# Moving the load of f to the head of the program and pinning twelve GpSimd loads in program order

## The chip, the cores and the metric

The kernel runs on one core of a Trainium2 chip. A core has TensorE (PE: matmuls, with its weight loads listed apart as PEld), VectorE (DVE), ScalarE (ACT), GpSimd (POOL) and SyncE (SP), each with a queue of its own that it works through in order, and sixteen DMA engines that all queues share. The metric is the device time of one execution in microseconds (us); lower is better.

## The reference

Inputs: q, k, v of shape (8, 8, 576, 64) for batch, head, position and head size; f of shape (8, 8, 576); w_in (512, 2048) and w_out (2048, 512).

```python
scores = q @ k.T / sqrt(64)
cum    = cumsum(log(clip(f, 1e-4, 1)), axis=-1)
scores = where(causal, -1e9, scores + cum[:, :, :, None] - cum[:, :, None, :])
attn   = softmax(scores) @ v
x      = attn with heads side by side, as 4608 tokens of 512
h      = x @ w_in
g      = h where h >= 1; 0 where h <= -1; (h + 1)**2 / 4 between
out    = g @ w_out
```

So the work is attention with a decay for each head, then two dense layers over all tokens.

## The kernel before

**Precision.** Later batches and the dense layers work on float16 pairs: a number is scaled by a power of two, its high part kept in one float16 and the rest in another, and a product takes three matmuls. The scale has to be known first: it comes from the largest absolute value of a whole batch of q, k or v. The first jobs work in float32 and need fewer scales.

**Jobs.** Attention is cut into 36 jobs, each two heads of one batch. Batch 0 has eight: its four head pairs with row blocks 0 and 1 (jobs 0 to 3), then with row blocks 2 to 4 (jobs 4 to 7). Batches 1 to 7 have four jobs each, with all five row blocks: batch 1 is jobs 8 to 11, batch 2 begins with job 12. Jobs below `NPE` = 8 turn their weights with PE in float32; jobs below `NQK` = 12 take q and k in float32, and from job 12 on q and k are split by a scale (`prepare`, L379).

**Loop.** The main loop (L737) walks the jobs. In job p it loads job p + 2, prepares job p + 1, and for each row block computes scores (`scores`, L443: PE writes them into PSUM, POOL lays out decay and causal mask at L474 and L478), the softmax (`weights`, L542: DVE takes the minimum at L556, ACT the exponential at L560, both split the result) and, in the second step, the product with v for the job before (`values`, L588, or `early_values`, L516). Between the steps it works off weight blocks (`weight_step`, L715: eight blocks of w_in and w_out are loaded by SP, their bits moved on DVE at L196 to L202, scaled and split; all in jobs 1 to 6) and units of the dense layers (`moe_unit`, L690: 256 tokens by one of eight weight blocks, 144 units in all). A unit can run only when all its tokens are through attention: chunk 0 after job 3, chunk 1 after job 7, chunks 2 and 3 after job 11.

**Start.** `decay_sums` (L140) loads f into the tile `early`, clips it on DVE (L144), takes the logarithm on ACT (L147), the running sum on DVE (L150), and stores it to DRAM as `cum_d`; `load_decay` (L369) reads it back, one row broadcast over all partitions. In the program, the load of f stands behind the loads of job 0's q and k (L362), all on SP's queue.

**The scales.** `value_scale(b)` (L236) loads a batch of v in four parts of 288 KB into `vm`, takes the largest absolute value of each on DVE (L245), and has `across` (L111) turn the result over the partitions with PE. `query_scale(b)` (L261) does it for q and k in eight parts (L268, L269). Batch 0's v is loaded by SP into another tile; all other parts are loaded by POOL into `vm`, which has two buffers that are used in program order: 28 loads for v of batches 1 to 7 and 48 for q and k of batches 2 to 7. In the program, `value_scale(1)` stands in job 7 behind the scores of its row block 4, and `query_scale(2)` in job 9 behind the scores of row block 1; v of batch 2 follows in job 11, q and k of batch 3 in job 13, and so on.

`across` uses the PSUM tile `s`, which has one buffer and is also that of the scores of row blocks 0 to 3. So this last step of a scale stays where the program has it, between two row blocks. The loads and the reductions before it do not: the small tiles that hold their results (`m4`, `m8`, `m1`, `m2q`, two buffers each) let them run some batches ahead.

**What sets the order.** The kernel is written for a scheduler (the context is opened with `schedule_with_timeline_sim=True`). It takes the instructions in the order in which the program issues them, simulates the engines, and fixes for each engine the order of its queue: an instruction whose inputs and buffers are free in that simulation may be put far ahead of its place in the program. On the chip each queue is then worked off in that fixed order, so an instruction that waits holds up everything behind it on its engine. `tc.keep_in_program_order(load)`, which the change calls, adds one condition to this: the load must be queued behind the instruction that the program issued last on the same engine before it. It is a condition of order alone; nothing waits for anything to end.

Of the kernel before, what the change touches and what calls it, by code (L numbers as in the profile page):

```python
# [30 lines left out]
NQK = 12  # L31
# [14 lines left out]
def kernel(  # L46
# [20 lines left out]
    nc = tc.nc  # L67

    B, H, S, D = q.shape
# [23 lines left out]
    early = xpool.tile([P, NPAIR, 2, S], F16, name="x").rearrange("p a b s -> p (a b s)").bitcast(F32)  # L93
# [11 lines left out]
    def scale_of(scale, power, m):  # L105

        nc.vector.tensor_scalar(out=power, in0=m, scalar1=1.0 / TOP, scalar2=None, op0=ALU.mult)
        even_pow2(power, power)
        nc.vector.reciprocal(scale, power)

    def across(dst, m):  # L111

        n = m.shape[1]
        pt = ps1.tile([P, 2, 512], F32, name="s")[:, 0]
        nc.tensor.transpose(pt[0:n, 0:P], m, ident)
        top = tiny.tile([P, 1], F32, name="top", bufs=2)  # L120
        nc.vector.tensor_reduce(out=top[0:n], in_=pt[0:n, 0:P], axis=AX.X, op=ALU.max)
        nc.vector.tensor_scalar(
            out=top[0:n], in0=top[0:n], scalar1=LOW, scalar2=HIGH, op0=ALU.max, op1=ALU.min
        )
        dg = tiny.tile([P, 2], F32, name="dg", bufs=2)
        nc.vector.tensor_scalar(
            out=dg[0:n, 0:n], in0=ident[0:n, 0:n], scalar1=top[0:n], scalar2=None, op0=ALU.mult
        )
        nc.tensor.matmul(pt[:, P:P + n], lhsT=ones[0:n], rhs=dg[0:n, 0:n], start=True, stop=True)
        nc.vector.tensor_copy(dst, pt[:, P:P + n])  # L130
# [6 lines left out]
    cum_d = dram.tile([B * H, S], F32, name="cum_d")  # L137
    cq8 = const.tile([P, NT5, B * H], F32, name="cq8")

    def decay_sums():  # L140
        fl = early
        nb = B * H
        nc.sync.dma_start(fl[0:nb, 0:S], f.rearrange("b h s -> (b h) s"))
        nc.vector.tensor_scalar(  # L144
            out=fl[0:nb, 0:S], in0=fl[0:nb, 0:S], scalar1=1e-4, scalar2=1.0, op0=ALU.max, op1=ALU.min
        )
        nc.scalar.activation(fl[0:nb, S:2 * S], fl[0:nb, 0:S], AF.Ln)  # L147
        nc.gpsimd.memset(fl[0:nb, 3 * S:4 * S], 0.0)
        cum = fl[0:nb, 2 * S:3 * S]
        nc.vector.tensor_tensor_scan(  # L150
            out=cum, data0=fl[0:nb, S:2 * S], data1=fl[0:nb, 3 * S:4 * S], initial=0.0, op0=ALU.add, op1=ALU.add
        )
        nc.sync.dma_start(cum_d, cum)
        pt = ps1.tile([P, 1024], F32, name="big")
        twice = fl[0:nb, 0:P]
        nc.vector.tensor_copy(
            twice.rearrange("p (a b) -> p a b", a=2), cum[:, FULL:S].unsqueeze(1).broadcast_to([nb, 2, 64])
        )
        for t in range(NT5):
            nc.tensor.transpose(  # L160
                pt[:, nb * t:nb * t + nb], cum[:, P * t:P * t + P] if t < LAST else twice, ident[0:nb, 0:nb]
            )
        nc.vector.tensor_scalar(
            out=cq8.rearrange("p t n -> p (t n)"), in0=pt[:, 0:NT5 * nb], scalar1=8.0, scalar2=None, op0=ALU.mult
        )
# [70 lines left out]
    def value_scale(b):  # L236
        m4 = tiny.tile([P, NPAIR], F32, name="m4", bufs=2)
        for i in range(NPAIR):
            if b:
                st = two.tile([P, S], F32, name="vm")  # L240
            else:
                st = stage[:, i * S:(i + 1) * S]
            part = v[b, 2 * i:2 * i + 2].rearrange("h s d -> (h s d)").rearrange("(p n) -> p n", p=P)
            (nc.gpsimd if b else nc.sync).dma_start(st, part)
            nc.vector.tensor_reduce(  # L245
                out=m4[:, i:i + 1], in_=st, axis=AX.X, op=ALU.max, apply_absolute_value=True
            )
        m1 = tiny.tile([P, 1], F32, name="m1", bufs=2)
        nc.vector.tensor_reduce(out=m1, in_=m4, axis=AX.X, op=ALU.max)
        m = mv[:, b:b + 1]  # L250
        across(m, m1)
        if b:
            nc.vector.tensor_tensor(out=m, in0=m, in1=mv[:, b - 1:b], op=ALU.max)
        scale_of(sv[:, b:b + 1], pv[:, b:b + 1], m)
# [6 lines left out]
    def query_scale(b):  # L261

        ms = tiny.tile([P, 2, NPAIR], F32, name="m8", bufs=2)
        for j, src in enumerate((q, k)):
            for i in range(NPAIR):
                st = two.tile([P, S], F32, name="vm")
                part = src[b, 2 * i:2 * i + 2].rearrange("h s d -> (h s d)").rearrange("(p n) -> p n", p=P)
                nc.gpsimd.dma_start(st, part)  # L268
                nc.vector.tensor_reduce(  # L269
                    out=ms[:, j, i:i + 1], in_=st, axis=AX.X, op=ALU.max, apply_absolute_value=True  # L270
                )
        m2 = tiny.tile([P, 2], F32, name="m2q", bufs=2)
        nc.vector.tensor_reduce(out=m2, in_=ms, axis=AX.X, op=ALU.max)
        mk = tiny.tile([P, 2], F32, name="mk", bufs=2)
        across(mk, m2)
        sc = sqk[:, :, b]
        scale_of(sc, mk, mk)
        nc.vector.tensor_scalar(
            out=nsig[:, b:b + 1], in0=sc[:, 0:1], scalar1=sc[:, 1:2], scalar2=-8.0, op0=ALU.mult, op1=ALU.mult
        )  # L280
        nc.vector.reciprocal(nalpha[:, b:b + 1], nsig[:, b:b + 1])
        nc.vector.tensor_scalar(
            out=cqs[b % 2], in0=cq8[:, :, b * H:(b + 1) * H], scalar1=nsig[:, b:b + 1], scalar2=-0.125,
            op0=ALU.mult, op1=ALU.mult,
        )
# [442 lines left out]

    pairs = [load(0)]
    decay_sums()  # L730
    pairs.append(load(1))
    load_decay(pairs[0], 0)
    load_decay(pairs[0], 1)
    prepare(pairs[0])
    value_scale(0)
    split_values(pairs[0])
    for p in range(njobs + 1):  # L737
# [3 lines left out]
        if w:  # L741
            if w.b not in xs:
                xs[w.b] = xpool.tile([P, NPAIR, 2, S], F16, name="x")
            if p + 2 < njobs:
                pairs.append(load(p + 2))
            if nxt:
                load_decay(nxt, 0)
                prepare(nxt)
            scores(w, w.r0)

            def step(r):
                if r + 1 < w.r1:
                    scores(w, r + 1)
                if r == w.r0 and w.hp == 1 and w.b + 1 < B and p + 3 >= NQK:
                    query_scale(w.b + 1)
                if r == w.r1 - 2 and nxt:
                    load_decay(nxt, 1)
                    if nxt.hp == 0 and nxt.r0 == 0:
                        value_scale(nxt.b)
                    split_values(nxt)  # L760
                weights(w, r)

            steps = [lambda r=r: step(r) for r in range(w.r0, w.r1)]
# [60 lines left out]
```

## Time and profile before

| what | value |
|---|---|
| median of 3 runs | 1199.87 us (1199.61 to 1200.08) |
| the profiled execution | 1195.69 us, its span 1193.9 us |
| PE | 1064.8 us busy, 89% |
| DVE | 806.8 us, 68% |
| ACT | 770.4 us, 65% |
| POOL | 476.1 us, 40% |
| mean granted clock of PE | 0.951 |
| loads into `vm` by POOL | 76, of 288 KB each |

The span runs from the first to the last instruction of the profiled execution; the time of an execution has a little more around it. Busy time counts an engine's own work, not its waiting or the issuing of transfers. In a row of a timeline stand the start, the duration, the engine, the line, the operation, the tiles (written <- read) and the shapes, the count, and in brackets how long the engine had been idle and what ended that. A row of waits has the waiting instruction, what it waited for, the total in us, how often, and the longest. In the rows of slices each digit is the busy share of a fortieth of the span in tenths; PEclk is the clock granted to PE in the same way. A chain of waits that the page follows from the last instruction back covers only the last 300 us here, which is dense work on PE; the first 330 us are therefore read by stretches.

### The profile page before, as it was taken

To read this page: it belongs to the slowest core of one execution; us is meant where nothing else is said; L and a number is where in the kernel's file an instruction comes from. 1 tells how busy PE (TensorE), PEld (TensorE's weight loads), DVE (VectorE), ACT (ScalarE), POOL (GpSimd) and SP (SyncE) were. 2 spreads that over 40 slices of the span, in tenths; PEclk is the share of its full clock that TensorE was granted. 3 is DMA by queue.
4 is the path that set the end of the run, shared out by engine and by line. 5 is a ranking of instruction groups with operands and counts; after the bars stand their busy time and mean duration, and the time that the engine had idled before them with its cause. 6 is when DMAs were issued, how large, how long until landed. Compare 5 with 4: busy or idle time off the path is not lost. (4 is left out here: it accounts for less than half of the span.)

```text
span 1193.9 us, 24608 instructions
## 1 busy us (share of the span) xinstructions
PE 1064.8 (89%) x8871; PEld 681.6 (57%) x8871; DVE 806.8 (68%) x2140; ACT 770.4 (65%) x1599; POOL 476.1 (40%) x811
## 2 busy tenths in 40 slices
PE   2566766998689899999999999999999999999998
PEld 1334443655356556655666665565566666677665
DVE  5979878777778777768656666777767866522222
ACT  2756555758567767777667666786777776644443
POOL 3588643534464544544432232454434444000000
PEclk9767888999789999999999999999999999999999
DMA  8797744689989977867665555777767773300000
GB/s 269 220 296 210 216 138 143 134 192 162 181 159 201 188 132 161 153 137 147 123 115 103 108 111 116 149 157 139 141 129 146 128 130 66 74 19 2 19 18 18
DMA packets 392537, 162.60 MB, mean 136 GB/s; under 512 B 370016, under 2 KB 371040, under 8 KB 392416
## 3 DMA queue, kind: packets, MB, share of 16 engines
q1 hardware_dynamic: 377312, 115.03, 49.4%
q0 software_dynamic: 9920, 36.58, 10.8%
q10 hardware_dynamic: 5184, 9.44, 2.3%
q8 instruction: 69, 1.13, 0.4%
q14 instruction: 52, 0.43, 0.1%
HBM read 89.80 MB, written 9.58 MB: 83 GB/s over the span
## 5 line engine op out<-in xcount | busy, mean ns | idle before, releaser
L637 PE MATMUL ph<-x,place 128*128 128x256 f16 (+3 forms) x4608 | 430.3, 248 | 10.1 <-DVE u L648 8.0
L665 PE MATMUL po<-place,g 128*128 128x512 f16 x1728 | 412.8, 382 | 4.1 <-ACT g L650 3.9
L637 PEld LDWEIGHTS <-place 128*128 128x128 f16 x4608 | 355.4, 99 | 85.4 <-issue 29.2
L474 POOL TENSOR_SCALAR sdr<-ck,nsig,cqs 128x128 f32<-128x128 f32 (+1 forms) x192 | 154.3, 808 | 297.7 <-DVE pr L575 278.5
L665 PEld LDWEIGHTS <-g 128*128 128x128 f16 x1728 | 162.3, 98 | 176.9 <-issue 8.3
L560 ACT ACTIVATE sdr<-sdr,nm 128x128 f32<-128x128 f32 (+1 forms) x240 | 132.6, 553 | 75.8 <-DVE nm L556 75.1
L648 DVE SCALAR_TENSOR_TENSOR u<-ph,z,u 128x512 f32<-128x512 f32 x136 | 101.5, 746 | 107.0 <-ACT u L647 106.7
L646 ACT ACTIVATE u<-ph,z 128x512 f32<-128x512 f32 x136 | 104.4, 768 | 80.0 <-PE ph L637 78.1
L650 ACT ACTIVATE g<-u,z 128x512 f16<-128x512 f32 x136 | 97.8, 719 | 71.0 <-DVE u L648 67.1
L575 DVE SCALAR_TENSOR_TENSOR pr<-sdr,rc,pr 128x128 f16<-128x128 f32 (+1 forms) x224 | 116.3, 555 | 39.9 <-ACT pr L574 37.7
L651 DVE SCALAR_TENSOR_TENSOR g<-u,z,g 128x512 f16<-128x512 f32 x136 | 104.2, 766 | 48.1 <-ACT g L650 47.6
L574 ACT ACTIVATE pr<-sdr,rc 128x128 f16<-128x128 f32 (+1 forms) x224 | 112.6, 550 | 18.9 <-ACT sdr L560 14.3
L556 DVE CUSTOM_DVE_ANT_0 sdr<-s,sdr,nalpha 128x128 f32<-128x128 f32 (+1 forms) x192 | 98.4, 546 | 26.5 <-PE s L466 16.2
L466 PE MATMUL s<-qkT 64*128 64x128 f16 (+5 forms) x704 | 88.3, 347 | 26.7 <-DVE nm L556 23.9
L595 PE MATMUL big<-pT,vs 128*64 128x64 f16 (+3 forms) x1008 | 83.8, 291 | 18.6 <-DMA pT<-pr 10.8
L647 ACT ACTIVATE u<-u 128x512 f32<-128x512 f32 x144 | 89.8, 624 | 2.5
L478 POOL TENSOR_SCALAR_AFFINE_SELECT sdr<-sdr 128x128 f32<-128x128 f32 x240 | 85.0, 363 | 7.8
L595 PEld LDWEIGHTS <-vs 128*64 128x64 f16 x1008 | 53.1, 113 | 51.6 <-issue 33.2
L474 POOL TENSOR_SCALAR sd<-ck,nsig,cqs 64x576 f32<-64x576 f32 x48 | 47.0, 980 | 78.9 <-DMA ck<-cum_d 60.5
L466 PEld LDWEIGHTS <-qkT 64*128 64x128 f16 (+1 forms) x864 | 32.8, 99 | 59.7 <-issue 46.1
L390 DVE SCALAR_TENSOR_TENSOR qs<-qk,sqk,qs 128x640 f16<-128x640 f32 x48 | 42.4, 910 | 30.8 <-ACT qs L389 30.8
L389 ACT ACTIVATE qs<-qk,sqk 128x640 f16<-128x640 f32 x48 | 37.3, 820 | 38.8 <-DMA qkT<-qs 33.2
(163 smaller groups left out, 1140.3 us busy)
## 6 DMA issues: line engine op xcount, KB each, us to landing
ck<-cum_d POOLq DMA_DIRECT2D x48, 288.0 KB, 4.5
out_dram<-ot ACTq DMA_DIRECT2D x36, 256.0 KB, 3.5
qk<-in_k_dram SPq DMA_DIRECT2D x64, 128.0 KB, 3.1
vm<-in_v_dram POOLq DMA_DIRECT2D x28, 288.0 KB, 3.5
v<-in_v_dram SPq DMA_DIRECT2D x56, 128.0 KB, 3.0
qk<-in_q_dram SPq DMA_DIRECT2D x56, 128.0 KB, 2.8
vm<-in_q_dram POOLq DMA_DIRECT2D x24, 288.0 KB, 3.4
vm<-in_k_dram POOLq DMA_DIRECT2D x24, 288.0 KB, 3.4
```

Source lines behind the costliest of these rows:

```text
L466: nc.tensor.matmul(outs[h][:, c0:c1], lhsT=x[rows], rhs=y[rows, c0:c1], start=(i == 0), stop=(i == len(terms) - 1),)
L474: nc.gpsimd.tensor_scalar(out=sd[p0:p1, 0:wid], in0=w.ck[h][p0:p1, 0:wid], scalar1=w.nsig if w.p < NQK else w.nsig[p0:p1], scalar2=w.cqs[p ...
L556: nc.vector.tensor_tensor_reduce(out=a, in0=sp, in1=a, scale=w.nalpha, scalar=BIG, op0=ALU.add, op1=ALU.min, accum_out=nm[:, i:i + 1],)
L560: nc.scalar.activation(a, a, AF.Exp, bias=nm[:, i:i + 1], scale=-1.0, accum_out=sm[:, i:i + 1])
L574: nc.scalar.activation(pr[:, :, 0, i, :], a, AF.Copy, scale=rc[:, i:i + 1])
L575: nc.vector.scalar_tensor_tensor(out=pr[:, :, 1, i, :], in0=a, scalar=rc[:, i:i + 1], in1=pr[:, :, 0, i, :], op0=ALU.mult, op1=ALU.subtract,)
L595: nc.tensor.matmul(av[64 * h:64 * h + 64, at + s0:at + s1], lhsT=w.vs[:, vl, h, t, :], rhs=w.pT[:, t, pl, h, s0:s1], start=(t == 0 and pi ...
L637: nc.tensor.matmul(ph[:, fi, a0:a1], lhsT=wi[fb][:, wl, t, fi * P:(fi + 1) * P], rhs=xs[b][:, t, xl, s0:s0 + a1 - a0], start=(fi == 0 and ...
L646: nc.scalar.activation(u, h, AF.Relu, scale=z.u[:, i:i + 1], bias=z.h[:, i:i + 1])
L648: nc.vector.scalar_tensor_tensor(out=u, in0=h, scalar=z.t[:, i:i + 1], in1=u, op0=ALU.max, op1=ALU.min)
L651: nc.vector.scalar_tensor_tensor(out=g[:, 1], in0=u, scalar=z.r[:, i:i + 1], in1=g[:, 0], op0=ALU.mult, op1=ALU.subtract)
L665: nc.tensor.matmul(po[ch][i], lhsT=g[:, gl, fi * TC + i * P:fi * TC + (i + 1) * P], rhs=wo[fb][:, wl, fi, :], start=(first and fi == 0 and ...
```

## The change

The load of f is issued as the first transfer of the program, ahead of the q and k of job 0. And twelve of the 76 loads into `vm` get the condition above: the four of v of batch 1, and the eight of q and k of batch 2 (`4 * (b + 1) == NQK` holds for b = 2). The other 64 are left to the scheduler, which lays out the order of all queues anew. Nothing is computed that was not computed before.

```diff
+    nc.sync.dma_start(early[0:B * H, 0:S], f.rearrange("b h s -> (b h) s"))
+
     def decay_sums():
         fl = early
         nb = B * H
-        nc.sync.dma_start(fl[0:nb, 0:S], f.rearrange("b h s -> (b h) s"))
...
-            (nc.gpsimd if b else nc.sync).dma_start(st, part)
+            load = (nc.gpsimd if b else nc.sync).dma_start(st, part)
+            if b == 1:
+                tc.keep_in_program_order(load)
...
-                nc.gpsimd.dma_start(st, part)
+                load = nc.gpsimd.dma_start(st, part)
+                if 4 * (b + 1) == NQK:
+                    tc.keep_in_program_order(load)
```

## The prediction

> **What bounds the kernel now.** I read the page first: the forty slices, then busy time by stretch.
>
> ```profile
> span 1193.9 us, 24608 instructions
> PE   2566766998689899999999999999999999999998
> DVE  5979878777778777768656666777767866522222
> PEclk9767888999789999999999999999999999999999
> ```
>
> One slice is 29.85 us. PE is far from full in the first seven slices, dips again in the eleventh, and is full from the twelfth on. Cut there:
>
> ```profile
> 0.00:223.00 223.00, 137.20 (x746) 89.51 (x747) 173.88 (x499) 124.24 (x304) 130.43 (x204) 0.82 0.71 210
> 223.00:334.00 111.00, 95.61 (x723) 57.01 (x720) 84.30 (x239) 73.76 (x159) 51.07 (x96) 0.92 0.87 169
> 334.00:1050.00 716.00, 692.63 (x6269) 439.83 (x6266) 508.52 (x1349) 511.54 (x1051) 294.64 (x512) 0.99 0.69 132
> 1050.00:1194.00 144.00, 139.32 (x1141) 95.22 (x1139) 40.09 (x54) 60.85 (x87) 0.00 (x0) 1.00 0.04 16
> ```
>
> (Stretch, its length, then busy us of PE, weight loads, DVE, ACT, POOL; granted clock; DMA share; GB/s.) From 334 us PE is busy 832.0 of 860 us: that part is as long as its matmuls. Before 334 us PE idles 101.2 us (334 - 137.2 - 95.6). So the run ends earlier or later by about as much as the attention of batches 0 and 1, which feeds PE, finishes earlier or later. In the first 223 us DVE is the fullest engine, 173.9 us. What the change moves is work of DVE, POOL and DMA in these two stretches: the `vm` loads and the reductions behind them.
>
> ```profile
> 0.00:100.00 100.00, 8.79 (x12) 7.61 (x13) 0.78 0.86 258
> 100.00:223.00 123.00, 29.84 (x40) 23.16 (x41) 0.85 0.59 172
> 223.00:330.00 107.00, 8.80 (x12) 6.83 (x12) 0.92 0.86 169
> 330.00:450.00 120.00, 8.87 (x12) 5.70 (x10) 0.94 0.84 170
> 2.64 1.27 POOL L244 DMA_DIRECT2D vm<-in_v_dram  x2
> 223.08 0.53 DVE L537 SCALAR_TENSOR_TENSOR x<-big,sv,x 128x320 f16<-128x320 f32 x1
> ```
>
> The first four rows are the same view for `vm` alone (busy us and count on DVE, then POOL). All 76 reductions are done by 450 us: 12, 40, 12, 12. Loads for batches that are attended hundreds of us later run ahead, the first pair at 2.64 us, and 40 of the reductions fall into the stretch at whose end, 223 us, batch 0 is finished (L537, the last step of job 7).
>
> **The change part by part.** The sum is made against the profiled execution: 1195.69 us, of which the span is 1193.9. It is 4.18 us under the median of the three runs, 1199.87; I add that at the end.
>
> *Load of f.*
>
> ```profile
> 0.75 0.97 SPq L362 DMA_DIRECT2D qk<-in_q_dram  x2
> 1.77 0.97 SPq L362 DMA_DIRECT2D qk<-in_k_dram  x2
> 2.79 0.57 SPq L143 DMA_DIRECT2D x<-in_f_dram  x1
> 7.59 0.45 DVE L144 TENSOR_SCALAR x<-x 64x576 f32<-64x576 f32 x1 [7.59 <-DMA x<-in_f_dram]
> 11.65 0.69 PE L408 MATMUL big<-ident,qk 128*128 128x128 f32 x2 [0.58 <-DVE cq L163]
> ```
>
> f moves past four loads of q and k on SP's queue, from 2.79 to 0.75 us: 2.04 us earlier, and DVE, which has done nothing until then, starts by as much earlier. The four loads go out 0.57 us later; the first transpose, which needs them, was released by DVE (cq) and not by them, so this is covered, unless f gains so much that q and k are next late. Taken: -2; ends 0 (the weight split on DVE, whose own loads stand behind on SP, is next late) and -4 (f's 4.8 us of landing shortens as well, since it no longer shares the engines with four loads).
>
> *The pinned loads: where they go.* A load of batch 1's v may now not stand ahead of the POOL instruction traced just before it, the last mask of row block 4 of job 7; the loads of q and k of batch 2 stand behind the second mask of row block 1 of job 9. Both can be found in POOL's timeline:
>
> ```profile
> 116.18 0.24 POOL L478 TENSOR_SCALAR_AFFINE_SELECT sd<-sd 64x64 f32<-64x64 f32 x1
> 235.03 0.29 POOL L478 TENSOR_SCALAR_AFFINE_SELECT sdr<-sdr 128x128 f32<-128x128 f32 x1
> ```
>
> So v of batch 1 starts at about 116 us, not at 2.64, and q and k of batch 2 at about 235. No other load is pinned, but all use the two `vm` buffers in program order, so all of them queue behind those twelve: none of the other 64 can start before about 250 us.
>
> *The first 100 us* lose 12 loads: 8.79 us of DVE, and POOL's waits for a buffer. DVE's longest waits there are not for them:
>
> ```profile
> DVE x L144 <- DMA x<-in_f_dram: 7.6, 1, 7.6
> DVE place L228 <- ACT place L223: 3.3, 2, 2.2
> DVE u L196 <- DMA place<-in_moe_w_out_dram: 3.2, 1, 3.2
> ```
>
> (Who waits for what, us in total, times, longest.) Ends 0 and -8.8; taken -2, near the first, because DVE's gaps there come from other work.
>
> *100 to 223 us* lose 40 reductions and get v's four.
>
> ```profile
> 100.00:223.00 123.00, 90.11 (x548) 59.32 (x549) 98.48 (x291) 71.06 (x162) 67.24 (x103) 0.85 0.59 172
> DVE m L269 <- DMA vm<-in_q_dram: 6.8, 5, 3.0
> DVE m L245 <- DMA vm<-in_v_dram: 4.3, 7, 1.6
> DVE m L269 <- DMA vm<-in_k_dram: 1.6, 4, 0.7
> ```
>
> DVE is busy 98.5 of 123 us, and stood still 12.7 us (6.8 + 4.3 + 1.6) at a reduction whose load had not landed, with the softmax and weight steps of batch 0 queued behind it. Reductions and stalls hold DVE 42.5 us. The gain is at most PE's idle time, 32.9 us (123 - 90.1), since PE's work stays; at least nothing. Taken: the stalls, 12.7, and a quarter of the 29.8 us of reductions (most fill time that DVE had to spare): -20. That is 0.5 us for each load. What is next late are the steps that PE waits for, exp and scaling on ACT. v's four loads cost 4 x 0.5 = +2.
>
> *Job 9.* The maxima of q and k of batch 2 are turned across partitions in the PSUM tile `s`, which has one buffer and passes from row block 1 of job 9 to these maxima and on to row block 2.
>
> ```profile
> 243.55 0.27 DVE L121 TENSOR_REDUCE top<-s 2x1 f32<-2x128 f32 x1
> 251.39 0.15 DVE L130 COPY mk<-s 128x2 f32<-128x2 f32 x1
> 253.50 0.92 PE L466 MATMUL s<-qkT 64*128 64x384 f32 x4
> vm<-in_q_dram POOLq DMA_DIRECT2D x24, 288.0 KB, 3.4
> L269 DVE TENSOR_REDUCE m<-vm x24: 716/745/754, 120.0 to 205.7; 128x1 f32<-128x576 f32 x24
> ```
>
> Before, their reductions were among the twelve of the first 100 us, and only the turn stood here. Now eight loads through two buffers take four rounds, each of landing 3.4, a second issue of 0.57 (as f's) and a reduction of 0.745, 4.7 us: 235.3 + 18.9 = 254.2, which is 10.6 after 243.55. Row block 2 of job 9, its softmax and all later scores are queued behind that. PE has units of chunk 1 to run meanwhile. Ends 0 (hidden: the turn itself was stretched over 7.8 us by other PE work) and +10.6; taken half, +5.
>
> A rule of the Trainium skill (DMA: Bandwidth & Descriptors, Rules for kernel authors) speaks against this part: a DMA should be issued early and waited for late, so that its fixed cost lies under compute. That page's fit, 2.0 us plus bytes over 436 GB/s, gives 2.7 us for 288 KB as an estimate, where this trace has 3.4; by it the lateness would be 7.8 us, and the sum -7 in place of -6.
>
> *After job 9.* The loads that were held back run ahead again. At the pace of 100 to 223 us (123 / 40 = 3.1 us each) 24 follow between 255 and 330 us; with q's and k's eight that makes 32 reductions where 12 were: 20 more.
>
> ```profile
> 223.00:330.00 107.00, 92.09 (x670) 54.12 (x668) 81.38 (x233) 72.12 (x156) 47.09 (x88) 0.92 0.86 169
> 330.00:450.00 120.00, 106.90 (x985) 68.69 (x984) 93.78 (x257) 82.71 (x178) 60.37 (x109) 0.94 0.84 170
> ```
>
> At the 0.5 us of before: +10. Ends: 0 (into gaps) and 20 x 1.06 = +21.3 (all of reduction and stall, 42.5 / 40, on the path). DVE without `vm` is busy 72.6 us here; 32 x 1.06 = 34.0 makes 106.6 of 107. It would be just full, and the DMA share is 0.86 already, against 0.59 where the burst lay before.
>
> *After 330 us* the other 40 (76 - 4 - 32) replace 12: 28 x 0.745 = 20.9 us of DVE, which has 26 us to spare beside a PE with 13.1 us idle. Taken +1; ends 0 and +13.1.
>
> Sum: -2 - 2 - 20 + 2 + 5 + 10 + 1 = -6. Profiled 1189.7; as a median of runs 1193.9.
>
> **The rivals.**
>
> *The burst does more harm where it goes (slower).* DVE full from 255 to 330 us, so that each of the 20 loads costs its 1.06 us, and job 9 waits its whole 10.6: -2 - 2 - 20 + 2 + 10.6 + 21.3 + 1 = +10.9, 1210.8. It decides once DVE's busy time and stalls in 223 to 330 us pass 107, or once the transposing DMAs of attention are late beside the loads. For it: DMA share 0.86, and PE idles 14.9 us (107 - 92.1) there, so it has no spare units for every wait. Against it: DVE has 25.6 us free there, and the pace of the burst falls if DVE is fuller.
>
> *Job 9's wait takes the place of the stalls (no change).* With all 10.6 us on the path and the rest as forecast, -0.4: 1199.5. By the rule of the Trainium skill named above (DMA: Bandwidth & Descriptors, Rules for kernel authors) a transfer issued late is exposed, and this would be the place. For it: one buffer of `s`, and every later score behind it. Against it: PE has chunk 1 to work on.
>
> *The pins hold nothing back.* They bind a load to one POOL instruction, and that may itself run early, as the one at 116 us does: the last step of job 7 is at 223 us. For job 9 that is unlikely, since the four `sdr` buffers hold its masks to 235 us. If so, only f is left: 1197.9. I count it under no change.
>
> **How the numbers follow.** What a measurement can tell from no change is about 0.2%, 2.4 us. The forecast and anything near it on the faster side has 0.61, no change 0.13, slower 0.26. The forecast's own range is 1176 (the stalls and half of the reductions gained early, -27.6; job 9 hidden; the burst at half its price: -2 - 2 - 27.6 + 2 + 0 + 5 + 1 = -23.6) to 1197. To leave out no more than 2 in 10 the range must hold the slower rival's middle too: 1176 to 1211.
>
> **What would show it.** Right: f issued at 0.75 and DVE's first work near 5.5 us; no `vm` load before about 100 us; the last step of batch 0 near 203 us in place of 223; 30 or more `vm` reductions between there and 330 us; PE as full as now from there on. Wrong: batch 0 done at 215 us or later (then the early reductions only filled gaps); a wait of PE for `mk` over 10 us in job 9; DVE's waits for `vm` landings in 220 to 330 us above 12 us; a PE that idles after 334 us by over 10 us more than now.

## The result, and the profile after

The changed kernel is slower: 1228.49 us in the median of 6 runs against 1199.74 for the kernel before. One of the six, at 1249.43 us, fell into a slower state of the chip and is left out of the ratio, which is 1.0254 (95% interval 1.022 to 1.0289). The profiled execution took 1233.49 us, its span 1231.6; it is 5 us over that median, and the one before lies 4 us under its own, so the two profiles are 38 us apart where the runs differ by 30. Differences between profiles below are read with that in mind. The page's slices after the change:

```profile
span 1231.6 us, 24631 instructions
PE   3766889883478879899999999999999999999998
DVE  5798667585667758778756576777766877622222
PEclk9866989897688989999999999999999999999999
DMA  8895205879999898987765466777776764400000
```

A slice is now 30.8 us. PE fills earlier than before (8 and 9 in slices five to seven), and then comes what was not there before: slices ten and eleven at 3 and 4, and no steady nine before the eighteenth. The DMA row tells where the transfers went: 2 and 0 in the fifth and sixth slice, then nines from the tenth to the thirteenth.

To follow this job by job, here is the end of some jobs (the last DVE step that writes the job's rows of x, in us from the span's start) in the profiled execution of the runs that are followed job by job below (each profile lies within 9 us of the median of its run):

| run | job 3 | 7 | 8 | 9 | 11 | 14 | 19 | 27 | 35 | span |
|---|---|---|---|---|---|---|---|---|---|---|
| before | 90 | 224 | 248 | 284 | 330 | 413 | 553 | 818 | 1044 | 1193.9 |
| the change | 71 | 195 | 225 | 285 | 348 | 466 | 591 | 856 | 1081 | 1231.6 |
| f_first_alone | 81 | 218 | 251 | 281 | 329 | 415 | 553 | 821 | 1046 | 1196.4 |
| pin_v1_alone | 71 | 209 | 244 | 282 | 338 | 417 | 564 | 829 | 1055 | 1205.7 |
| pin_qk2_alone | 83 | 195 | 225 | 285 | 343 | 452 | 593 | 862 | 1085 | 1235.7 |
| later_pinned | 81 | 198 | 225 | 253 | 306 | 408 | 569 | 844 | 1080 | 1229.5 |
| later_loads_eighth | 71 | 197 | 227 | 278 | 324 | 402 | 546 | 811 | 1036 | 1186.5 |
| later_reductions_eighth | 72 | 195 | 224 | 290 | 341 | 440 | 586 | 851 | 1079 | 1229.1 |
| qk2_one_job_earlier | 72 | 205 | 250 | 280 | 341 | 425 | 570 | 836 | 1061 | 1211.7 |
| later_loads_unread | 70 | 194 | 224 | 277 | 341 | 451 | 577 | 843 | 1067 | 1217.0 |
| paced_all | 71 | 203 | 234 | 270 | 316 | 406 | 556 | 851 | 1075 | 1225.3 |
| paced_all_late_maxima | 71 | 197 | 226 | 253 | 297 | 390 | 536 | 813 | 1042 | 1191.9 |

The second row against the first: 28 us gained by the end of batch 0 (job 7: 195.2 against 223.6), 6 us of it lost in job 8 and 23 in job 9 (59.5 us against 36.6), another 52 lost from job 10 to 14, some 15 won back by job 19, and then nothing moves. So the gain came, and nearly three times as much was lost behind it, all in the 270 us of jobs 8 to 14.

*The gain.* Busy time by stretch from 120 to 210 us (PE, weight loads, DVE, ACT, POOL, clock, DMA share, GB/s), before:

```profile
120.00:210.00 90.00, 63.03 (x374) 41.05 (x373) 72.42 (x214) 47.52 (x104) 42.10 (x65) 0.83 0.56 165
```

and after:

```profile
120.00:210.00 90.00, 78.05 (x517) 49.48 (x515) 60.54 (x198) 59.89 (x134) 25.15 (x42) 0.96 0.25 63
```

DVE does 12 us less, PE gets 15 us more done, and the DMA share falls from 0.56 to 0.25.

*Job 9.* The first load of q of batch 2 goes out right behind the mask that it is pinned to, as the timeline of POOL after shows:

```profile
211.03 0.29 POOL L483 TENSOR_SCALAR_AFFINE_SELECT sdr<-sdr 128x128 f32<-128x128 f32 x1
211.27 1.13 POOL L271 DMA_DIRECT2D vm<-in_q_dram  x2
...
231.26 0.59 POOL L271 DMA_DIRECT2D vm<-in_k_dram  x1 [3.23 <-DVE m L274]
235.39 0.54 POOL L271 DMA_DIRECT2D vm<-in_k_dram  x1 [3.54 <-DVE m L274]
```

On DVE the reductions wait for landings, and the turn of the maxima follows:

```profile
230.21 0.75 DVE L274 TENSOR_REDUCE m<-vm 128x1 f32<-128x576 f32 x1 [4.27 <-DMA vm<-in_k_dram]
234.34 0.75 DVE L274 TENSOR_REDUCE m<-vm 128x1 f32<-128x576 f32 x1 [2.71 <-DMA vm<-in_k_dram]
...
243.16 0.27 DVE L121 TENSOR_REDUCE top<-s 2x1 f32<-2x128 f32 x1
248.10 0.15 DVE L130 COPY mk<-s 128x2 f32<-128x2 f32 x1
```

The four rounds took 27.8 us, from 211.3 to the end of the last reduction at 239.1, and PE wrote the scores of row block 1 at 211.43 and those of row block 2 at 249.57: 38 us between two row blocks. Before, it was 15 us, from 238.42 to 253.50. First the row of row block 1 before, then both after:

```profile
238.42 0.70 PE L466 MATMUL s<-qkT 64*128 64x256 f32 x4
211.43 0.70 PE L471 MATMUL s<-qkT 64*128 64x256 f32 x4
249.57 0.92 PE L471 MATMUL s<-qkT 64*128 64x384 f32 x4
```

*After job 9.* The `vm` rows by stretch after the change, for the two stretches that the prediction used (DVE, POOL, clock, DMA share, GB/s; before they held 12 reductions each):

```profile
223.00:330.00 107.00, 25.52 (x34) 19.46 (x35) 0.81 0.93 190
330.00:450.00 120.00, 23.24 (x31) 17.42 (x31) 0.87 1.00 177
```

PE loses its time here by standing still. Jobs 10 to 15 before (284 to 440 us) and after (285 to 489), in the same columns as from 120 to 210:

```profile
284.00:440.00 156.00, 130.67 (x1162) 82.42 (x1160) 118.34 (x345) 104.27 (x228) 74.85 (x136) 0.90 0.89 175
285.00:489.00 204.00, 137.28 (x1186) 87.03 (x1185) 140.95 (x388) 110.07 (x238) 97.38 (x176) 0.84 1.00 183
```

Its busy time is 7 us more, its idle time 41 us more (25.3, then 66.7).

What the burst does to others shows in the DMA issues from 200 to 480 us: queue, count, size, median us to landing. Before:

```profile
v<-in_v_dram SPq DMA_DIRECT2D x22, 128.0 KB, 3.0
out_dram<-ot ACTq DMA_DIRECT2D x8, 256.0 KB, 3.8
pT<-pr SPq DMA_TRANSPOSE x56, 3.9
qkT<-qs SPq DMA_TRANSPOSE x8, 6.1
```

After:

```profile
out_dram<-ot ACTq DMA_DIRECT2D x6, 256.0 KB, 10.5
v<-in_v_dram SPq DMA_DIRECT2D x12, 128.0 KB, 8.9
pT<-pr SPq DMA_TRANSPOSE x46, 5.2
qkT<-qs SPq DMA_TRANSPOSE x6, 10.8
```

Every job from 12 on needs one `qkT` in its chain, and every job from 8 on six `pT`; they take 4.7 and 1.3 us longer. And DVE's waits in the same window (total, times, longest), after:

```profile
DVE m L274 <- DMA vm<-in_k_dram: 26.1, 15, 4.3
DVE m L274 <- DMA vm<-in_q_dram: 18.5, 12, 4.2
DVE m L248 <- DMA vm<-in_v_dram: 16.6, 12, 3.3
```

61.2 us; before the change the three made 6.6 us there. These are two candidates for the loss, the transfers and the waits, and the busy time of the reductions is a third. A fourth would be POOL, whose masks stand in its queue behind loads that wait for a buffer; but DVE waited 0.4 us for masks in this window, before the change 5.7, so that does not show. A profile can't tell which of them the time hangs on.

### The profile page after: what moved, and what is told of

It is laid out like the page before. It is cut to its first block, busy times and chain, and to the rows that moved or that the text cites. A ratio compares the mean times of both kernels' runs of the same rounds, so it can differ in the third digit from the quotient of the medians.

```text
span 1231.6 us, 24631 instructions
## 1 busy us (share of the span) xinstructions
PE 1073.8 (87%) x8871; PEld 686.2 (56%) x8871; DVE 809.0 (66%) x2140; ACT 769.2 (62%) x1599; POOL 474.8 (39%) x811
## 5 line engine op out<-in xcount | busy, mean ns | idle before, releaser
L642 PE MATMUL ph<-x,place 128*128 128x256 f16 (+3 forms) x4608 | 435.8, 250 | 18.1 <-DVE u L653 13.0
L642 PEld LDWEIGHTS <-place 128*128 128x128 f16 x4608 | 359.8, 99 | 96.1 <-issue 35.1
L471 PE MATMUL s<-qkT 64*128 64x128 f16 (+5 forms) x704 | 92.8, 360 | 51.3 <-DVE nm L561 44.3
L274 DVE TENSOR_REDUCE m<-vm 128x1 f32<-128x576 f32 x48 | 36.0, 750 | 44.8 <-DMA vm<-in_k_dram 26.1
```

The costliest lines, as they stand in the source:

```text
L471: nc.tensor.matmul(outs[h][:, c0:c1], lhsT=x[rows], rhs=y[rows, c0:c1], start=(i == 0), stop=(i == len(terms) - 1),)
L642: nc.tensor.matmul(ph[:, fi, a0:a1], lhsT=wi[fb][:, wl, t, fi * P:(fi + 1) * P], rhs=xs[b][:, t, xl, s0:s0 + a1 - a0], start=(fi == 0 and ...
```

## The experiments

Theory 1 is the burst behind job 9, theory 2 the late maxima in job 9, theory 3 a bad draw of the order.

**f_first_alone.** The change without the two pins.

```diff
-            if b == 1:
-                tc.keep_in_program_order(load)
...
-                if 4 * (b + 1) == NQK:
-                    tc.keep_in_program_order(load)
```

> The load of f first, no load pinned. Theory 1 (the burst: what was held back runs ahead all at once behind job 9, and its transfers and reductions fall on attention's own): nothing is held back, so 2 us faster, 1196 to 1200. Theory 2 (job 9: the maxima of q and k of batch 2 come late, and all later work behind them): the same. Theory 3 (any edit gives a new order of all queues, and this one is a bad draw): anything from 1190 to 1215.

Measured 0.9954 of before (0.9924 to 0.9984). The first part of the change is a small gain, a few us more than the 2 that theories 1 and 2 named; the whole loss, and more, comes from the pins.

**pin_v1_alone, pin_qk2_alone.** One of the pins each, with f first.

> f first and only the four loads of v of batch 1 pinned. All 72 other loads then start behind about 110 us and not behind 210 us. Theory 1: they fall on the end of batch 0 and on jobs 8 to 10, less densely than with both pins: 1200 to 1215. Theory 2: the maxima of q and k of batch 2 are done before job 9 again, so 1195 to 1200.

> f first and only the eight loads of q and k of batch 2 pinned; v of batch 1 may run ahead. Theories 1 and 2 both expect what both pins give, 1222 to 1232, with batch 0 done near 197 us: the four loads of v are not the cause. A time below 1212 would speak for theory 3.

Measured 1.013 (1.009 to 1.0171) and 1.0344 (1.0297 to 1.039). With v alone pinned, the 72 loads behind it start at 117 us in place of 19; batch 0 is 15 us earlier, and by job 19 the kernel is 11 us behind. The maxima of q and k of batch 2 are not late there (the last of their reductions is done at 140 us), so theory 2 can't explain it; theory 1 named the size. With q and k alone pinned, jobs 7 to 9 end as with the change (195, 225, 285), and the loss behind them is there too; the median, 1239.48, is 7 us above what theories 1 and 2 named.

**all_pinned, later_pinned.** All 76 loads pinned; and the pins turned round, on all but the twelve of the change (`b > 1` for v, `b > 2` for q and k).

> f first and all 76 loads into vm pinned, so none runs ahead of its place. Theory 1: no burst; batch 0 done near 195 us as with the change, job 15 no later than before (438 us), total 1175 to 1195. Theory 2: the wait of job 9 comes back in each of jobs 13, 17, 21, 25 and 29, so as slow as the change or slower, 1225 to 1250.

> f first; the pins turned round: v of batch 1 and q and k of batch 2 may run ahead as before, the 64 loads of all later batches are pinned. Theory 1: no burst and no late maxima in job 9, and the stretch from 100 to 223 us loses its 40 reductions: batch 0 done near 200 us, total 1170 to 1190. Theory 2: job 9 as before, but a wait of its kind in each of jobs 13 to 29: 1200 to 1230.

Measured 1.0523 (1.0464 to 1.0583) and 1.0288 (1.0253 to 1.0323). Both lie on the side of theory 2, a little beyond its figures, and theory 1 was wrong on both. The table shows why for later_pinned: without late maxima job 9 takes 28 us (225 to 253) and job 11 ends 24 us earlier than before; then each batch whose loads stand at their place in the program loses: from job 14 to job 27 it takes 436 us, before 405.

**later_loads_eighth, later_reductions_eighth.** The change, with the 64 later loads and their reductions cut to an eighth of the columns; and with the loads whole but the reductions cut.

```diff
-                load = nc.gpsimd.dma_start(st, part)
+                n = S // 8 if b > 2 else S
+                load = nc.gpsimd.dma_start(st[:, 0:n], part[:, 0:n])
...
-                    out=ms[:, j, i:i + 1], in_=st, axis=AX.X, op=ALU.max, apply_absolute_value=True
+                    out=ms[:, j, i:i + 1], in_=st[:, 0:n], axis=AX.X, op=ALU.max, apply_absolute_value=True
```

> The change, with the 64 loads of later batches (v from batch 2 on, q and k from batch 3 on) cut to an eighth of their columns, and their reductions too; the scales come from that eighth. It leaves out seven eighths of the bytes and of the reduction time of the burst, and keeps job 9's loads whole. Theory 1: 1175 to 1195. Theory 2: as slow as the change, 1220 to 1232.

> The change, with the 64 later loads whole but their reductions over an eighth of the columns. Only the DVE time of the burst is left out. If the burst costs by its DVE time, as I priced it, 1190 to 1205; if by its transfers (landings that DVE waits for, and attention's own transfers that are late), 1215 to 1230. Theory 2: 1220 to 1232.

Measured 0.9915 (0.9883 to 0.9948) and 1.0216 (1.0153 to 1.0279). The first keeps the change's pins and the late maxima of job 9 (51 us from 227 to 278), and the loss behind job 9 is gone: job 14 ends at 402 in place of 466. So the bytes of the 64 loads, with their reductions, cost 0.034 of the time, about 41 us (0.0339 x 1199.7). The second shows that the busy time of the reductions is at most a small part of that: the two intervals, with and without it, overlap, and DVE's waits for landings stay (68.7 us from 200 to 480 us, where the change has 61.2). That leaves DVE's waits for landings and the transfers of others.

**later_loads_unread.** The eighths again, brought by loads of their own into a tile of their own, and the 64 whole loads beside them that nothing reads.

```diff
+                if b > 2:
+                    nc.gpsimd.dma_start(st, part)
+                    st = two.tile([P, S // 8], F32, name="vm8")
```

> The change, with the 64 later loads whole, but nothing reads them: the reductions read an eighth of the same rows that a second small load brings into a tile of its own. Against the run with eighths alone (1188) it adds only the bytes, and no DVE wait for them. If the burst costs by attention's own transfers that are late beside it: 1212 to 1230. If it costs by DVE standing at a reduction whose load has not landed: 1186 to 1200.

Measured 1.0213 (1.017 to 1.0256), so 0.030 over the eighths. The rows of its DMA issues and of DVE's waits from 200 to 480 us:

```profile
out_dram<-ot ACTq DMA_DIRECT2D x6, 256.0 KB, 6.3
pT<-pr SPq DMA_TRANSPOSE x48, 5.7
qkT<-qs SPq DMA_TRANSPOSE x6, 11.5
```

```profile
DVE m L282 <- DMA vm<-in_k_dram: 12.6, 9, 2.0
DVE m L282 <- DMA vm<-in_q_dram: 7.6, 6, 3.5
DVE m L252 <- DMA vm<-in_v_dram: 3.0, 4, 1.2
```

The same of the run with the eighths:

```profile
pT<-pr SPq DMA_TRANSPOSE x58, 4.4
qkT<-qs SPq DMA_TRANSPOSE x8, 5.9
```

```profile
DVE m L276 <- DMA vm<-in_k_dram: 12.6, 11, 3.0
DVE m L276 <- DMA vm<-in_q_dram: 12.3, 13, 2.5
DVE m L249 <- DMA vm<-in_v_dram: 7.4, 9, 2.1
```

DVE waits 23.2 us for landings here and 32.3 with the eighths alone, so it doesn't wait more; but attention's transposes are as late as with the change. (The burst is as dense as the change's: 72 of the whole loads go out from 200 to 480 us in both, 34 of them before 305 us here and 31 there.) ACT, which can write the next `qs` only when `qkT` has been made from the last one, waits for that. In the same window here, with the eighths, with the change and before:

```profile
ACT qs L402 <- DMA qkT<-qs: 39.6, 6, 12.0
ACT qs L396 <- DMA qkT<-qs: 11.0, 6, 4.8
ACT qs L394 <- DMA qkT<-qs: 23.0, 5, 7.3
ACT qs L389 <- DMA qkT<-qs: 16.4, 7, 5.7
```

So bytes that nothing reads bring back nearly the whole loss, and in this run they do it beside attention's transfers and not through DVE's waits; nor through POOL, which issues 64 loads more, for DVE waits 0.8 us for its masks (1.0 with the eighths). With the change itself ACT's wait is only 7 us longer than before, and DVE's waits for landings 55 us, so there the two can share the loss in another way. The Trainium skill states that such transfers share their engines (DMA: Bandwidth & Descriptors, Issuing engines are not separate DMA queues): those started by SP, ACT and POOL run on the same sixteen and interleave. The trace agrees: with POOL's unread loads beside them, SP's `qkT` went from 5.9 to 11.5 us and `pT` from 4.4 to 5.7. SP's 128 KB loads of v, which took 8.9 us with the change, took 4.4 in this run; why they were so late with the change stays open.

**qk2_one_job_earlier.** The change, with `query_scale(2)` traced in job 8.

```diff
-                if r == w.r0 and w.hp == 1 and w.b + 1 < B and p + 3 >= NQK:
+                if r == w.r0 and w.hp == (0 if w.b == 1 else 1) and w.b + 1 < B and p + 4 >= NQK:
```

> The change, with the maxima of q and k of batch 2 traced in job 8 and not in job 9, pins and all. Theory 1: the burst only starts a job earlier, 1218 to 1230. Theory 2: the wait is moved off job 9 to a place of the same kind, so what it costs moves with it: job 8 late by as much as job 9 was, and the total again 1220 to 1232, or less if batch 0 has more units left to cover it.

Measured 1.0096 (1.0067 to 1.0126), less than theory 1 expected; theory 2 had left a lower time open. The wait moved, as theory 2 has it: job 8 takes 45 us (205 to 250) and job 9 30. But the loads now begin at 154 us, where the DMA engines were idle with the change (a share of 0.07 from 150 to 180 us), and jobs 10 to 14 take 145 us in place of 181. Moving wait and burst forward by one job was worth 19 us of the total (1.0254 to 1.0096).

**paced_later, paced_all.** An attempt to keep the early gain. Loads and reductions are taken out of `value_scale` and `query_scale` and traced one to a row block, twelve to a batch, pinned; from job 8 on, or from job 4 on with v of batch 1 and q and k of batch 2 among them.

```diff
                 weights(w, r)
+                if w.p >= pace_from and ahead and (w.p - 4) % NPAIR * (w.r1 - w.r0) + r - w.r0 < 3 * NPAIR:
+                    ahead.pop(0)()
```

> f first; v of batch 1 and q and k of batch 2 free as before; the 64 later loads pinned, but traced one at a time, one to a row block, from job 8 on, 12 in the first 12 row blocks of each batch, well ahead of the step that needs their maxima. No burst and no wait as in job 9. Expected from the run with all later loads pinned in place: job 11 ends near 306 us as there, and from then on the pace of before (job 35 then ends 714 us later): 1165 to 1185. If every order but the old one is worse (theory 3), over 1200.

> The same, with the twelve loads of v of batch 1 and q and k of batch 2 paced as well, one to a row block in jobs 4 to 7. The first 100 us are then free of them (job 3 ends near 71 us and not 81), batch 0 ends near 197 us, job 9 has no wait and ends near 253: 1160 to 1185. If theory 2's wait is only moved, job 9 takes over 50 us again and the total is over 1195.

Measured 1.0205 (1.0171 to 1.0239) and 1.028 (1.0248 to 1.0312), 37 and 46 us over the upper ends of what was expected. paced_all is ahead of before up to job 14 (406 against 413) and loses from there on, 29 us of it from job 19 to 27, where before has no `vm` loads at all: 294 us in place of 265. No burst is left and no late maxima. DVE's waits from 480 to 900 us:

```profile
DVE m L282 <- DMA vm<-in_k_dram: 18.0, 9, 4.5
DVE m L282 <- DMA vm<-in_q_dram: 14.2, 6, 3.6
DVE m L252 <- DMA vm<-in_v_dram: 10.7, 8, 2.7
```

42.9 us, while the kernel before has none there. I read this so: the scheduler puts the reduction on DVE's queue where its simulation has the load landed; on the chip it lands later, and DVE stands. (No run shows the simulation's own times.) That reading called for one more pair.

**paced_all_late_maxima, dense_early_late_maxima.** The reduction is traced one row block after its load and pinned to DVE's order; and with that, two loads to a row block in jobs 4 to 7 and then three to a job.

```diff
+                while tops:
+                    tops.pop(0)()
                 if w.p >= pace_from and ahead and (w.p - 4) % NPAIR * (w.r1 - w.r0) + r - w.r0 < 3 * NPAIR:
-                    ahead.pop(0)()
+                    tops.append(ahead.pop(0)())
```

> As with all loads paced, but the reduction of a load is traced one row block after the load and pinned to DVE's order there, so that DVE reaches it when the load has long landed. The bytes, their places and the number of reductions stay. If in sparse loads the price is DVE standing at a reduction (74 us of such waits with all loads paced, 19 before): those waits fall below 10 us and the total to 1160 to 1185. If it is the bytes beside attention's transfers: 1215 to 1232 as before the edit.

> The same late maxima, but two loads to a row block in jobs 4 to 7, where the DMA share with the change falls to 0.28 and 0.07, so 24 loads there, and then three to a job, a batch ahead of need. If loads are cheapest where the DMA engines are idle, this is as fast as one to a row block or faster, 1160 to 1185, with batch 0 done by 205 us; if a load costs the same 0.7 us wherever it lies, batch 0 ends near 212 us and the total is 8 us over the paced one.

Measured 0.9899 (0.9873 to 0.9926) and 1.0006 (0.9979 to 1.0034). The first took 0.038 off paced_all with every byte and every reduction kept. From 480 to 900 us one row of such waits is left in it:

```profile
DVE m L253 <- DMA vm<-in_v_dram: 2.8, 2, 2.4
```

while `pT` landed in 5.0 us from 200 to 480 us, no sooner than the 4.5 of paced_all. So for sparse loads the price was mainly DVE standing at reductions that were queued too early. This is the lowest ratio of all, 1% under before; f alone, which is in it too, gives about half of that (0.9954). dense_early_late_maxima gave no difference from before, and is no faster than one load to a row block: its guess, that loads are cheap wherever the DMA engines are idle, did not hold as a rule, and what it loses against the paced one was not taken apart.

Theory 3, that every order but the old one is worse, had the figure that it named in paced_later (over 1200); against it are two other orders that do all the work and are faster than before, f_first_alone (0.9954) and paced_all_late_maxima (0.9899). But each edit lays out all queues anew, and no run shows how much of a difference between two of them is the new order and not the thing edited.

## Why the prediction was wrong

*The load of f* went as described, and further: DVE began at 3.74 us in place of 7.59, not at 5.5, because f landed 3.0 us after its issue and not 4.8. Alone it is worth 0.46%, about 5.5 us (2 to 9), where the term was -2 with an end at -4.

*Where the pins put the loads* was right: behind masks that ended at 99.8 and 211.3 us (foreseen 116 and 235, without what the change itself gains before them).

*The first 223 us* came near the sum: -22 foreseen for both stretches with f and v, -28 measured at job 7. The runs take it apart. f alone ends job 7 6 us earlier (217.6 against 223.6); later_pinned, which beside f clears the stretch from 100 to 223 us of all but one of its reductions, 25.5 us (198.1); the change 28.4. That is 6 for f, 19.5 for those loads and 3 for the other twelve, where -2, -20 and 0 (-2 + 2) were foreseen. So the largest term held. Whether its 19.5 us are reductions and stalls of DVE, as the prediction has it, or transfers beside those of batch 0, no run shows.

*Job 9* was right in place and mis-sized. The term was +5 with an end at +10.6, from rounds of 4.7 us at the median landing. The rounds took 7 us each: two of the loads of k landed 7 and 10 us after their issue, beside attention's transposes. Job 9 took 59.5 us: 23 more than before, and 32 more than where the maxima were in time (27.5 in later_pinned). The rule of the Trainium skill that stood beside it (DMA: Bandwidth & Descriptors, Rules for kernel authors: issue early, wait late) was the better guide here, and the trace agrees with it. But the early loads had had a price too: holding them back, with f first, gained 28 us by the end of batch 0.

*"After job 9" and "After 330 us"* are the steps that failed. They priced 48 loads more than before at +10 and +1, ends +21.3 and +13.1. Jobs 10 to 14 lost 52 us, and with the later loads cut to an eighth that loss is gone (job 14 at 402 us in place of 466). The price for one load had been taken from 100 to 223 us, where the DMA share was 0.59, and the bound from DVE's busy time and waits there; it was carried to a place where the share was 0.86 and every job hangs on DMA transposes. After 330 us I compared 20.9 us of reductions with DVE's 26 spare us: the wrong resource, as later_reductions_eighth and later_loads_unread show. And the end there, +13.1, was PE's idle time, which bounds what can be gained and not what can be lost: in jobs 10 to 15 that idle time grew by 41 us. Of the prediction's own signs of being wrong, DVE's waits for `vm` landings over 12 us from 220 to 330 us came true, with 31.5 us. The slower rival had the cause among its conditions ("once the transposing DMAs of attention are late beside the loads") but took its price, and so its 1210.8, from DVE alone.

*From job 19 on* the kernel takes as long as before (641 us to the end of the span in both), as forecast: what is lost before PE is full stays lost.

How the change's loss behind job 9 divides between the late transposes and DVE's 61 us of waits is not settled: the unread loads cost nearly as much (1.0213 against 1.0254, with intervals that overlap) without more waits of DVE, but ACT's wait for `qkT` is 39.6 us there and 23.0 with the change, and they come with 64 small loads that the change does not have.

## What to carry to other kernels

Prefetches that run ahead have a price where they lie, and here holding them back moved it to a place where it was higher: before pinning a load, look at what the DMA engines do at the place where it will land, not only at the place that it leaves. Here other work on the critical path went through DMA there, the cost came with the bytes, and DVE's spare time did not show it. And on an engine that works in order, it paid here to queue the consumer of a load later than the scheduler would: one row block of distance turned a loss of 2.8% into a gain of 1%.

## What the runs showed that I had not expected

Transfers were not all slowed alike where the DMA share went to 1.00: with the change the loads of v on SP's queue went from 3.0 to 8.9 us (4.4 beside as many unread loads) and the output stores from 3.8 to 10.5, `qkT` from 6.1 to 10.8, `pT` only from 3.9 to 5.2, and the loads of q into `vm` stayed at 3.9 (4.0 before) where those of k took 5.6 (3.3). And a sparse load cost about 1.2 us of the kernel's time (29 us for the 24 loads from job 19 to 27 in paced_all) although its reduction is 0.75 us and DVE had time to spare. Three fifths of it went when the reduction was queued later: there the same jobs took 277 us, against 294 and the 265 of a stretch without loads. That profile is the slowest of its six runs, 8.5 us over their median, so this may be more.
